# Message passing on a graph: the chunks of 8 tiles end at sorting step 36 instead of 140

## The chip, the cores and the metric

The kernel runs on one core of a Trainium2 chip. Its engines work side by side, each through its own list of instructions in order: TensorE (PE; its weight loads are shown as PEld), VectorE (DVE), ScalarE (ACT), GpSimd (POOL, which here issues the indirect DMAs) and SyncE (SP, which issues the plain DMAs). They wait for one another through semaphores. The metric is the time of one execution on the device in microseconds (us).

## The reference: what is computed

A graph has 12,500 nodes with 64 features and 800,000 edges with 16 features. Each edge takes the features of its source, of its destination and its own, multiplies them with a weight matrix, and applies SiLU; the messages are summed by destination, and each node is updated from its features and its sum.

```python
m_in = jnp.concatenate([x[src], x[dst], e_attr], axis=-1)
msg = _silu(m_in @ w_msg)
agg = _segment_sum(msg, dst, N)
return _silu(jnp.concatenate([x, agg], axis=-1) @ w_upd)
```

Sources and destinations are drawn at random, so edges come in no order, and the sum is by destination.

## The kernel before, in words

**Two halves that run side by side.** The first half sorts edges by destination into 128 buckets of 98 nodes. A tile is 128 edges; there are 6250 of them. The sorted records (17 numbers: 16 edge features, and one that packs source and position) go to a store in device memory, `st`. The second half reads whole tiles of one bucket back, forms the messages, and adds them into the accumulator `ACC`.

**Sorting step.** There are 782 steps of 8 tiles (`M`). A step goes through a pipeline of periods, one stage a period: `onehot` (ACT makes a one-hot matrix of the buckets, lines 396 and 397) and `sums` (running sums over the tiles of a chunk, lines 403 to 412, mostly DVE); then `count` (PE, lines 425 to 428, into the only PSUM tile `z`), `ranks` (DVE, line 433: each edge's rank in its bucket) and `expand` (DVE, lines 442 to 446: each record is put at its rank's place in a wide row of `X`); then `move` (PE, line 463: one-hot matrix times `X`, which adds the tiles of a chunk up in the only PSUM tile `pl`). When a chunk is complete, ACT copies the block out (line 468), and `place` (DVE, lines 481 and 482) moves the buckets' pointers on. In the period after, POOL scatters the block to the store (line 486), one row to each bucket.

**Chunks.** A chunk is the set of tiles whose ranks are counted together and which make one scatter. The first `K8 = min(N8, ...)` chunks have 8 tiles, one step and one scatter each (`turn` 3). All later chunks have 12 tiles: three steps hold two chunks, and `turn` 0, 1, 2 says which of the three a step is. A row of `X` for the tile at position n of its chunk has room for `LIM[n]` records, so that the moving operand of line 463 has `2 + 17 * LIM[n]` columns, and the scattered row of a bucket has the room of the chunk's last tile:

```python
LIM = [k for k in (13, 17, 21, 24, 27, 30) for _ in range(2)]
S = LIM[-1]
S8 = LIM[M - 1]
```

That gives 223, 223, 291, 291, 359, 359, 410, 410 columns for a chunk of 8, and 461, 461, 512, 512 more for the last four tiles of a chunk of 12. In turn 1 a chunk ends after the step's fourth tile: `move(0)` does four tiles, then comes the product of the other half, then `move(1)` does four tiles of the next chunk. The running sums go on over the border of a step inside a chunk of 12: turns 0 and 2 need two additions (lines 409 and 410) where a chunk of 8 has one (412), and turn 2 needs a third count matmul for both of its halves (line 428); the others need it for one.

**Groups and batches.** The second half works on groups of tiles, and a group is fed to the pipeline in batches. A group takes units of `u` tiles of one bucket, and there are three stages, by the line

```python
FIRST = [(1, 48, BT, (1, 0, 1, 0)), (2, 24, 6, (3, 3, 2, 2))]
```

First units of 1 in batches of 8 (64 tiles in all), then units of 2 in groups of 24 and batches of 6 (640 tiles), then units of 4 (`QU`) in groups of 64 and batches of 8; in the end units of 1 for what is left, and the last, part-filled tiles. A group is formed over several periods: DVE works out from the pointers which tiles it takes (`fourth`, lines 545 to 563), with two small PE passes (`middle`, lines 581 and 585 to 587), then SP loads the tiles from the store into `rt` (line 569), and DVE takes the indices out (`fifth`, line 530). For the groups of the first two stages (`quick`) the first PE pass stands inside the period's main stream: PE waits there for DVE's `wl`. A batch then takes one period for each of: `gather` (POOL, line 649: one indirect DMA a tile fetches the sources' rows into one of four buffers `g`) and its one-hot matrix (DVE 659, ACT 660); `transpose` (PE 668, ACT 671) and `product` (PE 677); `message` (DVE 681, ACT 682); `reduce` (PE 698) and `add` (DVE 706 or 710).

**The order of work.** The order within a period is written out by hand in `period` (lines 715 to 773): POOL gets four gathers, then the scatter, then the rest of the gathers; PE gets `count`, `transpose`, `reduce`, `move(0)`, `product`, `move(1)`; DVE gets the batch's one-hot, `ranks`, `message`, `add`, `sums`, `expand`, `place`.

**The planner.** When a group may begin is decided when the program is made, with no knowledge of the data. `Draws` keeps sixteen drawn examples of how full the buckets are, from a generator with a fixed seed; `holds` asks whether the least full of them has enough whole units; `place(Chunk(i).m)` adds a chunk's tiles to them when the chunk is placed. A period for which no group is ready has no batch. When all steps are done, the remaining batches run alone, at the end.

The number of chunks also sets how many tiles of the store each bucket owns (`CAPT`), where the last chunk's empty tiles lie (`T1`, `GAP`), and the size of the table `LOST`, which would list chunks where a bucket had more records than room; such chunks would be done again at the end.

Of the kernel before, what the change touches and what calls it, by code (L numbers as in the profile page):

```python
# [21 lines left out]
MAGIC = 12582912.0  # L22
M = 8
C = 12
N8 = 140
LIM = [k for k in (13, 17, 21, 24, 27, 30) for _ in range(2)]
S = LIM[-1]
S8 = LIM[M - 1]
# [20 lines left out]
def mpnn_kernel(tc, x, e_attr, src, dst, w_msg, w_upd, out):  # L49
# [4 lines left out]
    assert E % P == 0 and NB <= NBK and NT >= C  # L54
    K8 = min(N8, NT // (2 * M))
    NCH = K8 + (NT - K8 * M + C - 1) // C
# [1130 lines left out]
```

## Time and profile before

| what | value |
|---|---|
| median of 3 runs | 10888.96 us (10887.72 to 10916.87) |
| the profiled execution's own time | 10887.83 us |
| its span | 10886.0 us |
| the last sorting step's rank reduction starts | 10036.8 us |
| gathers, scatters | 6322, 567 (and one to another pointer) |
| busy share of the span: PE, DVE, ACT, POOL | 82%, 66%, 47%, 60% |

The profile is one execution. Times are counted from the start of its span. A row for a stretch gives its length, then each engine's busy time and the number of its instructions in it, then the mean TensorE clock that was granted (1.00 is full), the DMA engines' busy share and GB/s; where the row is of one line's instructions, the engines' times are of these alone. A row of a group gives line, engine, operation, output and inputs, shapes, count, busy time and mean duration in ns, and then the engine's idle time just before, with what ended it. A row in order of time gives start, duration, engine, line, operation, how many were merged, and in brackets the idle time before it. Matmuls are pipelined, so that start to start tells more of them than a duration.

### The profile page before, as it was taken

Reading aid. Unit: us, or ns where it says so; the run is one execution under the profiler, and the core shown is the slowest. Engines: PE = TensorE matmul, PEld = TensorE weight load, DVE = VectorE, ACT = ScalarE, POOL = GpSimd, SP = SyncE. Lnnn points to the kernel's source line nnn. Section 1 sums busy time; section 2 is a strip of 40 time slices with the busy share of each in tenths; the row PEclk is TensorE's granted clock in tenths of the full one; section 3 lists DMA queues with packets and bytes.
Section 4 is the critical chain, followed back from the end, with each engine's and each line's share of the span. In section 5 each row is a group of like instructions: output and inputs, shape, how many; then the busy total and the mean of one; then the engine's idle time right before and its main releaser. Section 6 shows DMA issues by size and latency. Waiting matters only on the chain. (4 is left out here: it accounts for less than half of the span.)

```text
span 10886.0 us, 155616 instructions
## 1 busy us (share of the span) xinstructions
PE 8949.9 (82%) x49053; PEld 6219.2 (57%) x49816; DVE 7231.4 (66%) x15936; ACT 5082.6 (47%) x12594; POOL 6571.4 (60%) x6908
## 2 busy tenths in 40 slices
PE   8788888888888888888888888888888888888556
PEld 5566655555555555555555555555555555555555
DVE  7777776666666666766666666666666666766232
ACT  6455554444444444444444444444444444544211
POOL 2565666666666666666666666666666666666555
PEclk9999998999989988999998999999899998988555
DMA  3111111111111111111111111111111111111212
GB/s 97 44 49 48 49 49 46 43 47 42 47 42 46 45 44 45 44 43 44 46 43 46 44 44 43 46 47 43 45 42 46 43 47 44 44 45 41 46 36 44
DMA packets 662903, 501.15 MB, mean 46 GB/s; under 512 B 492983, under 2 KB 529911, under 8 KB 662071
## 3 DMA queue, kind: packets, MB, share of 16 engines
q0 software_dynamic: 238976, 349.72, 12.3%
q1 hardware_dynamic: 422775, 141.27, 5.9%
q8 instruction: 400, 6.55, 0.3%
q14 instruction: 432, 3.54, 0.1%
q10 hardware_dynamic: 320, 0.07, 0.0%
HBM read 330.05 MB, written 152.30 MB: 44 GB/s over the span
## 5 line engine op out<-in xcount | busy, mean ns | idle before, releaser
L649 POOL DMA_INDIRECT g<-A_d,sidx x6322 | 5997.6, 949 | 3658.7 <-issue 1620.7
L463 PE MATMUL pl<-X,hf 128*128 128x291 f32 (+5 forms) x12512 | 4745.0, 524 | 476.4 <-issue 428.3
L463 PEld LDWEIGHTS pl<-X,hf 128*128 128x128 f32 x12512 | 2538.7, 211 | 2159.4 <-issue 1737.4
L446 DVE TENSOR_TENSOR X<-cb,rec 128x442 f32<-128x442 f32 (+5 forms) x3128 | 2646.6, 908 | 26.7
L396 ACT ACTIVATE hf<-iof,shi 128x128 f32<-128x128 f32 x6256 | 1908.8, 389 | 1360.4 <-PE pl L463 449.0
L671 ACT ACTIVATE qt<-tq 114x1024 f32<-114x1024 f32 (+1 forms) x818 | 811.7, 992 | 2951.3 <-remote 2298.5
L433 DVE TENSOR_REDUCE rank<-z 128x8 f32<-128x1024 f32 x782 | 954.5, 1221 | 1270.3 <-remote 874.9
L677 PEld LDWEIGHTS pre<-w,qt 114*128 114x128 f32 x10496 | 1392.5, 209 | 687.8 <-ACT qt L671 467.1
L677 PE MATMUL pre<-w,qt 114*128 114x64 f32 x10496 | 1395.2, 291 | 345.6 <-ACT qt L671 317.6
L710 DVE TENSOR_TENSOR ACC<-ag,ACC 64x98 f32 x1938 | 496.7, 256 | 1553.3 <-remote 1131.7
L698 PE MATMUL ag<-q,g 128*64 128x98 f32 x12644 | 882.3, 276 | 490.4 <-remote 236.2
L698 PEld LDWEIGHTS ag<-q,g 128*64 128x64 f32 x12644 | 681.6, 151 | 668.8 <-issue 381.7
L668 PE MATMUL tq<-ident,q 128*114 128x128 f32 x6322 | 929.9, 294 | 103.3 <-issue 91.5
L668 PEld LDWEIGHTS tq<-ident,q 128*114 128x114 f32 x6322 | 812.6, 147 | 238.7 <-issue 122.6
L397 ACT ACTIVATE hf<-hf,ones 128x1024 f32<-128x1024 f32 x782 | 898.8, 1149 | 25.4
L486 POOL DMA_INDIRECT st<-blk,ptrs x567 | 567.2, 1000 | 561.4 <-ACT blk L468 272.2
L659 DVE TENSOR_TENSOR q<-cb,lo 128x784 f32<-128x784 f32 (+1 forms) x818 | 768.7, 940 | 96.1 <-PE ag L698 46.3
L468 ACT ACTIVATE blk<-pl 128x512 f32<-128x512 f32 (+1 forms) x568 | 324.9, 572 | 818.2 <-PE pl L463 500.9
L426 PE MATMUL z<-G,onesb 128*128 128x384 bf16 x1564 | 529.8, 339 | 78.9 <-issue 25.2
L682 ACT ACTIVATE g<-g 128x512 f32<-128x512 f32 (+1 forms) x818 | 498.4, 609 | 192.5 <-DVE g L681 111.8
L681 DVE TENSOR_TENSOR g<-pre,g 128x512 f32<-128x512 f32 (+1 forms) x818 | 541.3, 662 | 51.4 <-issue 37.2
L677 PE MATMUL pre<-BW,qt 114*128 (+1 forms) x2148 | 326.3, 314 | 99.0 <-ACT qt L671 64.8
(138 smaller groups left out, 5243.9 us busy)
## 6 DMA issues: line engine op xcount, KB each, us to landing
g<-A_d,sidx POOLq DMA_INDIRECT x6322
ea<-in_e_attr SPq DMA_DIRECT2D x260, 192.0 KB
rt<-st SPq DMA_DIRECT2D x1312, 34.0 KB
st<-blk,ptrs POOLq DMA_INDIRECT x567
rt<-st SPq DMA_DIRECT2D x434, 8.5 KB
nodes<-in_x SPq DMA_DIRECT2D x62, 98.0 KB
ACC<-rt SPq DMA_DIRECT2D x11, 544.0 KB
rt<-st SPq DMA_DIRECT2D x320, 17.0 KB
```

The costliest lines, as they stand in the source:

```text
L396: nc.scalar.activation(c.hf[:, k, :], iof, AF.Square, bias=c.hi[:, k:k + 1])
L397: nc.scalar.activation(c.hf, c.hf, AF.Relu, bias=ones, scale=-1.0)
L433: nc.vector.tensor_reduce(out=c.rank, in_=c.z, axis=AX.X, op=OP.max)
L446: nc.vector.tensor_tensor(out=c.x[:, k:k + 2, 2:2 + n * R].rearrange("p k (s c) -> p k s c", c=R), in0=hit[:, k:k + 2, 0:n, None].to_broad ...
L463: nc.tensor.matmul(pl[:, 0:w], c.hf[:, k, :], c.x[:, k, 0:w], start=(n == (c.size - 1 if whole else 0)), stop=ends, skip_group_check=True)
L486: i = nc.gpsimd.indirect_dma_start(out=st, out_offset=bass.IndirectOffsetOnAxis(ap=c.ptr, axis=0), in_=c.blk[:, 2:], in_offset=None)
L649: j = nc.gpsimd.indirect_dma_start(out=t.g[:, i, :], out_offset=None, in_=A_d, in_offset=bass.IndirectOffsetOnAxis(ap=t.grp.sidx[:, k:k + ...
L659: nc.vector.tensor_tensor(out=t.q[:, 0:n, 0:BK], in0=ioB[:, None, :].to_broadcast([P, n, BK]), in1=t.grp.lo[:, i0:i0 + n, None].to_broadca ...
L668: nc.tensor.transpose(t.tq[0:KQ, j * P:(j + 1) * P], t.q[:, j, :], ident)
L671: nc.scalar.activation(t.qt[:, 0:w], t.tq[0:KQ, 0:w], AF.Copy)
L677: nc.tensor.matmul(t.pre[:, i * D:(i + 1) * D], t.qt[:, i * P:(i + 1) * P], w, start=True, stop=True)
L698: o = nc.tensor.matmul(t.ag[t.half(v), v // 2 * BK:(v // 2 + 1) * BK], t.g[:, i, :], t.q[:, i, 0:BK], start=(k == 0), stop=(k == u - 1))
```

## The change

`N8`, the number of chunks of 8 tiles at the start, goes from 140 to 36:

```diff
 M = 8
 C = 12
-N8 = 140
+N8 = 36
 LIM = [k for k in (13, 17, 21, 24, 27, 30) for _ in range(2)]
```

Steps 0 to 35 stay as they were. Steps 36 to 139 now belong to chunks of 12 and go through turns 0, 1 and 2, as the later steps do. There are 533 chunks instead of 568, and so 35 scatters fewer. The steps are 782 as before; the last one has 4 tiles. A bucket owns 125 tiles of the store instead of 128, and `LOST` has 533 columns. The planner's draws are made in other portions.

## The prediction

> **What bounds the kernel now.** I read the page first (engine shares, slices), then tables by stretches of time with the instructions of one line alone, then lists in order of time. The page names no single full engine:
>
> ```profile
> span 10886.0 us, 155616 instructions
> PE 8949.9 (82%) x49053; PEld 6219.2 (57%) x49816; DVE 7231.4 (66%) x15936; ACT 5082.6 (47%) x12594; POOL 6571.4 (60%) x6908
> ```
>
> The change touches the sorting steps 36 to 139, so the stretch that matters is found by counting steps. Each sorting step has one rank reduction (L433). Its rows for three stretches (the stretch, its length, busy time, count, granted TensorE clock, DMA share, GB/s):
>
> ```profile
> 600.00:1400.00 800.00, 87.64 (x72) 0.92 0.20 49
> 1700.00:9700.00 8000.00, 735.12 (x602) 0.91 0.17 45
> ...
> 355.80:1519.40 1163.60, 126.57 (x105) 0.92 0.20 50
> ```
>
> A step takes 800/72 = 11.1 us in the first stretch, where chunks have 8 tiles, and 8000/602 = 13.3 us in the second, where they have 12. The third stretch runs from the reduction of step 36 to that of step 140: 104 steps, 11.2 us each. These are the steps that the change rewrites. It is tempting to say that each will then cost 13.3 us (104 x 2.1 = +218 us), but the two stretches differ in something else too, the gathers (L649):
>
> ```profile
> 600.00:1400.00 800.00, 410.13 (x431) 0.92 0.20 49
> 1700.00:9700.00 8000.00, 4564.05 (x4814) 0.91 0.17 45
> ```
>
> 431/72 = 6 gathers a step early, 4814/602 = 8 later: the early batches belong to the second stage of groups, with 6 tiles a batch, and that stage is not touched. So the change makes a kind of step that the profile hardly has: chunks of 12 with batches of 6. What the two extra tiles cost must come out of the 2.1 us.
>
> All engines over the same two stretches (length; PE, PEld, DVE, ACT, POOL busy):
>
> ```profile
> 600.00:1400.00 800.00, 665.30 (x3734) 487.28 (x3806) 612.01 (x1607) 418.56 (x1031) 482.17 (x503) 0.92 0.20 49
> 1700.00:9700.00 8000.00, 6745.60 (x36911) 4577.32 (x37513) 5492.84 (x11580) 3859.84 (x9629) 4966.48 (x5216) 0.91 0.17 45
> ```
>
> In the early stretch PE is busy 83% and VectorE 77% of the time: PE leads, VectorE is close behind. ScalarE (52%) has room.
>
> **The change part by part.** *TensorE, the moves (L463).* A move of 8 tiles sends 2 x (223+291+359+410) = 2566 columns; three moves with chunks of 12 send 2 x 2 x (223+291+359+410+461+512) = 9024, or 3008 each: 442 more a step. PE in order of time, two early steps with chunks of 8 (start, us, line, count):
>
> ```profile
> 1096.57 4.58 PE L463 MATMUL pl<-X,hf 128*128 128x410 f32 x16
> 1100.99 1.45 PE L677 MATMUL pre<-BW,qt 114*128 x12
> ...
> 1103.06 0.38 PE L428 MATMUL z<-G,onesb 128*128 128x512 bf16 x1
> 1103.27 0.82 PE L668 MATMUL tq<-ident,q 128*114 128x128 f32 x6
> 1104.02 0.89 PE L698 MATMUL ag<-q,g 128*64 128x98 f32 x12
> 1104.84 4.58 PE L463 MATMUL pl<-X,hf 128*128 128x410 f32 x16
> ```
>
> The move starts at 1096.57 and the product at 1100.99: 4.42 us, 1.72 ns a column; 442 more columns are 0.76 us. The crossover at step 140 has, for a moment, what the change makes common, three moves of chunks of 12 beside batches of 6:
>
> ```profile
> 1536.87 3.53 PE L463 MATMUL pl<-X,hf 128*128 128x461 f32 x8
> 1540.24 1.45 PE L677 MATMUL pre<-BW,qt 114*128 x12
> 1541.53 1.95 PE L463 MATMUL pl<-X,hf 128*128 128x223 f32 x8
> 1543.32 0.39 PE L425 MATMUL z<-hf,w 128*128 128x512 bf16 x1
> ...
> 1545.65 6.11 PE L463 MATMUL pl<-X,hf 128*128 128x359 f32 x16
> 1551.60 1.00 PE L677 MATMUL pre<-BW,qt 114*128 x8
> ```
>
> From start to the next start: 3.37 + 1.79 = 5.16 us for the second move of a turn, 5.95 for the third; the first has the columns of a chunk of 8 (4.42). Mean 5.18, again 0.76 more. The split move also shows that waiting for the only `pl` buffer between its halves is hidden behind the product.
>
> *TensorE, the counts.* One step in three has a third-term matmul (L428) more; 1103.06 to 1103.27 is 0.21 us, a third is 0.07. TensorE: **+0.83 us a step**. As a check, two more tiles cost 2 x (0.75/6 + 1.29/6 + 0.82/6) = 0.95 us by the starts above, and 0.83 + 0.95 = 1.8 of the 2.1 us between the two kinds of step. So step time follows TensorE's work.
>
> *VectorE.* The expansions (L446), by the same two stretches, and the small groups, over the whole run (count | busy us, mean ns):
>
> ```profile
> 600.00:1400.00 800.00, 214.99 (x286) 0.92 0.20 49
> 1700.00:9700.00 8000.00, 2086.87 (x2408) 0.91 0.17 45
> ```
>
> ```profile
> L412 DVE TENSOR_TENSOR G<-G,hf 128x128 bf16<-128x128 bf16 x568 | 174.3, 307 | 19.5
> ...
> L409 DVE TENSOR_TENSOR cb<-G,hf 128x128 f32<-128x128 bf16 x428 | 126.8, 296 | 7.3
> L482 DVE SCALAR_TENSOR_TENSOR ptrs<-blk,LOST,ptrs 128x1 int32<-128x1 f32 x567 | 125.9, 222 | 20.1
> L410 DVE TENSOR_TENSOR G<-cb,G 128x128 bf16<-128x128 f32 x428 | 124.6, 291 | 14.6
> ...
> L481 DVE SCALAR_TENSOR_TENSOR LOST<-blk 128x1 f32<-128x1 f32 x568 | 86.9, 153 | 95.9 <-ACT blk L468 83.3 <-issue 11.8
> ```
>
> Four expansions a step: 214.99/286 x 4 = 3.01 us against 2086.87/2408 x 4 = 3.47: +0.46. Running sums: one L412 (0.307) becomes two thirds of L412, L409 and L410 each, 2/3 x 0.894 = 0.596: +0.29. A third of the L481 and L482 pairs goes: -0.125. VectorE: **+0.63 us a step**. One block copy in three goes from ScalarE; it has room, so this counts nothing.
>
> *POOL.* 69 or 70 of 104 scatters stay, 35 go. POOL in order of time:
>
> ```profile
> 1109.05 0.94 POOL L649 DMA_INDIRECT g<-A_d,sidx  x1 [2.00 <-remote]
> ...
> 1114.06 1.00 POOL L486 DMA_INDIRECT st<-blk,ptrs  x1 [0.30 <-issue]
> ```
>
> A scatter holds POOL for 1.00 + 0.30 us (the pause before each), a gather for about 0.95 + 0.30, so a step loses 0.43. POOL's work in an early step is 6 x 1.25 + 1.30 = 8.8 of 11.1 us, and each batch's first gather waits (2.00 us here), so I book nothing; if POOL were the bound, this would be a gain of 45 us (a rival below). The scatters' bytes fall too (two thirds of 2040 against 1632 bytes a partition), in DMA engines with a 0.20 share: nothing.
>
> *Waits.* No wait is added. The group that is being formed makes PE wait for VectorE's `wl` once in a group (PE in order of time):
>
> ```profile
> 1115.91 0.38 PE L581 MATMUL cb<-wl,tri 128*128 128x1 f32 x2 [3.94 <-DVE wl L546]
> ```
>
> Groups have 24 tiles, 4 batches of 6, so this is one step in four. There VectorE's chain sets the end, and it grows by 0.63; in the other three PE's 0.83 counts. Mean (3 x 0.83 + 0.63)/4 = 0.78 us; **104 x 0.78 = +81 us**. Ends for one step: -0.43 (POOL bounds all) and +1.56 (below); I take 0.78 as it lies at the rows of the stage itself.
>
> *The plan of groups.* The planner sees no run-time data: its draws come from a generator with seed 1. Worked through by its own arithmetic for 140 and 36, both have 847 periods and 818 batches, and the same 29 periods without a batch (0 to 24, 33 to 36), so no batch moves to the end. Two differences: two groups of the second stage begin at steps 49 and 51, not 47 and 49, and the last group of 64 tiles with a unit of 4 becomes one with a unit of 1. The first may let VectorE wait for loads into `rt`; all such waits of 117 groups are 13.8 us:
>
> ```profile
> L530 DVE CAST sidx<-rt 128x64 int32<-128x64 f32 x117 | 33.5, 286 | 33.7 <-DMA rt<-st 13.8 <-issue 13.5 <-DMA g<-A_d,sidx 3.3
> ```
>
> I take +3 (0 to 13.8). The second is priced by the message additions (L681) in the tail, units of 4 and then of 1:
>
> ```profile
> 10070.00:10260.00 190.00, 9.64 (x14) 0.55 0.23 47
> 10280.00:10860.00 580.00, 30.40 (x45) 0.57 0.23 40
> ```
>
> 13.6 us a batch against 12.9: 8 batches, -5 us (0 to -10). The last step has 4 tiles instead of 8: half a move, -3. By the inputs as they are drawn no bucket of any chunk passes its limit before or after (after twelve tiles at most 28 of 30), so the path for lost records does not run.
>
> *Sum.* 81 + 3 - 5 - 3 = +76 us on the profiled execution's 10887.83, which stands 1.1 below the median of 10888.96: **10965 us**.
>
> **A rule beside a row.** PE's wait of 3.94 us has a tail. Before it and just after it (columns as for all engines):
>
> ```profile
> 1089.40:1116.60 27.20, 23.07 (x136) 17.18 (x138) 21.69 (x51) 15.74 (x40) 17.81 (x19) 1.00 0.26 66
> 1116.60:1120.00 3.40, 3.40 (x18) 2.38 (x17) 1.29 (x4) 0.89 (x2) 1.35 (x2) 0.50 0.12 24
> ```
>
> For 3.4 us the granted clock is 0.50, which costs 1.7 us of TensorE time. The Trainium skill, "TensorE: Matmul & The Clock Gate", section on what is actually happening in Part 1, says that the clock falls to half after an idle window of about 3.4 us and comes back after a busy one, and that the windows run freely. The trace agrees in size and place. It is a mechanism by which more TensorE work could cost less (third rival).
>
> **Rivals.** *POOL is what steps wait for* (faster). For it: the two kinds of step differ by two gathers, 2 x 1.25 - 0.43 = 2.1 us of POOL, as well as 1.8 us of PE. Against it: POOL itself waits at a batch's first gather. It decides if those waits are only a shadow of POOL's own lateness; then 104 x -0.43 = -45: 10844. *It is hidden*: PE is idle 17% of the stage, 1.9 us a step, and 0.8 could go into that: about 10885. Against it: the waits are for VectorE, which gets more work too. *Fewer half-clock windows*: PE's wait falls by 0.83 - 0.63 = 0.20, to 3.7 us; if that makes it miss a window in each of 26 groups, 26 x 1.7 = 44 us come back: 10921. *The move is slower than its columns say.* L463 over the two stretches (PE busy, PEld busy):
>
> ```profile
> 600.00:1400.00 800.00, 355.22 (x1148) 224.56 (x1149) 0.92 0.20 49
> 1700.00:9700.00 8000.00, 3800.97 (x9628) 1968.01 (x9629) 0.91 0.17 45
> ```
>
> 4.95 against 6.32 us a step, +1.37, and with the counts about +1.56: 104 x 1.56 = +162, 11050. Against it: the crossover's moves had their plain length. *The change doesn't do what it says*, in that steps stay without a batch: each would add about 13 us at the end; the plan above has none.
>
> **How the numbers follow.** Chances: forecast 0.67 (10935 to 10995 by itself), slower move 0.08, fewer windows 0.07, hidden 0.11, POOL 0.07. A change of 0.3% (33 us) is about what a measurement of this kernel tells from none. Faster is POOL, 0.07; same is hidden and a part of fewer windows, 0.13; slower is the rest, 0.80. The range leaves out POOL, the lower half of hidden, and most of slower move: 10890 to 11010.
>
> **What would show it.** Right: the 104 steps take 11.9 to 12.0 us; scatters fall from 567 to 532; early moves average 5.2 us from start to next start; L409 and L410 appear before 1400 us; the stage with 8 tiles a batch stays at 13.3. Wrong: early steps at 10.8 (POOL), at 11.2 (hidden), or above 12.5, or a later stretch whose steps change.

## The result, and the profile after

The changed kernel takes 10919.3 us (median of 14 runs, 10891.79 to 10941.12) beside 10901.2 for the kernel before (14 runs): a ratio of 1.0014, with a 95% interval of 1.0004 to 1.0024. That is 15 to 18 us where 76 were forecast: less than the 0.3% that the prediction names as what a measurement tells from none, though inside the range given. The profiled execution took 10907.74 us. The head of its page:

```profile
span 10905.8 us, 155764 instructions
## 1 busy us (share of the span) xinstructions
PE 8991.1 (82%) x49079; PEld 6205.4 (57%) x49842; DVE 7300.5 (67%) x16020; ACT 5068.6 (46%) x12543; POOL 6526.7 (60%) x6873
```

PE and DVE have more to do, POOL less, as the change says. The rewritten steps 36 to 139, all engines over the stretch (length; PE, PEld, DVE, ACT, POOL busy; granted clock, DMA share, GB/s), first the kernel before, then the changed one:

```profile
355.80:1519.40 1163.60, 964.66 (x5381) 703.83 (x5483) 885.58 (x2324) 605.45 (x1490) 704.69 (x735) 0.92 0.20 50
```

```profile
357.70:1514.50 1156.80, 1016.24 (x5406) 692.08 (x5508) 949.67 (x2354) 598.67 (x1456) 668.95 (x700) 0.93 0.21 47
```

Here the sum of the prediction falls. PE has 52 us more to do, DVE 64, POOL 36 less, and the 104 steps take 11.1 us each: 7 us *less* in all, where +81 was forecast. What the whole loses, it loses after the last step. The gathers (L649) from the last rank reduction on, in three stretches (length, POOL busy, count), before and after:

```profile
10036.80:10086.80 50.00, 30.26 (x32) 0.76 0.14 34
10086.80:10286.80 200.00, 113.44 (x120) 0.55 0.24 49
10286.80:10886.00 599.20, 334.59 (x354) 0.57 0.23 40
```

```profile
10018.80:10068.80 50.00, 18.31 (x20) 0.83 0.15 40
10068.80:10268.80 200.00, 112.68 (x120) 0.54 0.22 39
10268.80:10905.80 637.00, 349.66 (x371) 0.59 0.26 41
```

This tail took 849.2 us and now takes 887.1. In its first 250 us the changed kernel starts 140 gathers, the kernel before 152. With +2 before step 36 and -13 between step 140 and the last one, +2 - 7 - 13 + 38 = +20 is the difference of the two profiled spans.

### The profile page after: what moved, and what is told of

Its sections match the earlier page's. It is cut to its first block, busy times and chain, and to the rows that moved or that the text cites. A ratio compares the mean times of both kernels' runs of the same rounds, so it can differ in the third digit from the quotient of the medians.

```text
span 10905.8 us, 155764 instructions
## 1 busy us (share of the span) xinstructions
PE 8991.1 (82%) x49079; PEld 6205.4 (57%) x49842; DVE 7300.5 (67%) x16020; ACT 5068.6 (46%) x12543; POOL 6526.7 (60%) x6873
## 5 line engine op out<-in xcount | busy, mean ns | idle before, releaser
L649 POOL DMA_INDIRECT g<-A_d,sidx x6322 | 5988.9, 947 | 3723.2 <-issue 1648.6
L463 PE MATMUL pl<-X,hf 128*128 128x410 f32 (+5 forms) x12504 | 4802.1, 529 | 467.4 <-issue 428.7
L446 DVE TENSOR_TENSOR X<-cb,rec 128x442 f32<-128x442 f32 (+5 forms) x3126 | 2692.8, 923 | 26.6
L433 DVE TENSOR_REDUCE rank<-z 128x8 f32<-128x1024 f32 x782 | 954.0, 1220 | 1121.4 <-remote 780.9
L486 POOL DMA_INDIRECT st<-blk,ptrs x532 | 531.2, 999 | 556.9 <-ACT blk L468 276.1
```

Source lines behind the costliest of these rows:

```text
L433: nc.vector.tensor_reduce(out=c.rank, in_=c.z, axis=AX.X, op=OP.max)
L446: nc.vector.tensor_tensor(out=c.x[:, k:k + 2, 2:2 + n * R].rearrange("p k (s c) -> p k s c", c=R), in0=hit[:, k:k + 2, 0:n, None].to_broad ...
L463: nc.tensor.matmul(pl[:, 0:w], c.hf[:, k, :], c.x[:, k, 0:w], start=(n == (c.size - 1 if whole else 0)), stop=ends, skip_group_check=True)
L649: j = nc.gpsimd.indirect_dma_start(out=t.g[:, i, :], out_offset=None, in_=A_d, in_offset=bass.IndirectOffsetOnAxis(ap=t.grp.sidx[:, k:k + ...
```

## The experiments

A word ahead, since it decides how the numbers are read. The runs were made in sets, each set on one chip, and the sets are of two kinds. In three of them the kernel before took 10720, 10894 and 10728 us, like the first measurement (10901); in two others the same kernel took 8912 and 8926. I call a chip of the first kind late and one of the second early, for a reason that is shown further down. The names stand for what was seen in a set: the sets at 10894 and at 8912 us are on record under the same chip number. Ratios are always to the kernel before in the same set, and stages are compared within one kind, between sets in which the kernel before took about the same time.

**The tail alone.** Two kernels exchange the last group of 64 tiles and nothing else. First the changed kernel with the group of units of 4 kept (5952 tiles up to there), then the kernel before without it (5888):

```diff
-        large = work["used"] + max(0, draws.sure(QU) * QU // GT * GT) if state["u"] == QU else 0
+        large = 5952
...
+        large = 5888
```

> The changed kernel, but the last group of 64 tiles with units of 4 is kept (93 groups up to there, as before the change), so that one group of units of 1 goes. Theory 'the tail costs it': the stretch from the last rank reduction (849.2 us before the change, 887.1 after) falls by 25 to 40 us to about 850, and the time to about 10880, 20 below the kernel before; steps 36 to 139 stay at 11.1 us. Rival 'the tail differs by chance or by its starting state': it stays at 870 to 890 us and the time at about 10919.

> The kernel before (N8 = 140), but its last group of 64 tiles with units of 4 is given up for one with units of 1, as the change does. Theory 'the tail costs it': the stretch after the last rank reduction rises from 849 to about 885 us, the time to about 10937, and steps 36 to 139 stay at 11.2 us. Rival 'chance or starting state': 850 us and 10901.

The first stood at 1.0007 (0.9997 to 1.0018) with a tail of 852.1 us, the second at 1.0026 (1.0016 to 1.0036) with a tail of 865.0. On the same kind of chip, the one other kernel with chunks of 8 and the group of units of 4 (it leaves out gathers in early steps, next part) had 829.2, and the changed sorting with units of 1 had 864.6 and 864.2. So giving the group up costs the kernel before +28 us by its ratio and 36 by these two tails; keeping it gives the changed kernel back only some 12 to 18 us (852.1 and 846.3 against 864). What keeps its tail 17 to 23 above 829 was not separated; in the sets near 10900 us, three profiles of chunks of 8 with that group differ by 12 us among themselves (849.2, 857.6, 861.2).

**POOL and its transfers.** The scatters that go had been booked at nothing. One kernel gives the changed one a gather in each period that lost its scatter, into a buffer that nobody reads; another takes a gather away from every third early step of the kernel before (the second part of the diff):

```diff
+            elif q and 38 < flow["ic"] <= 142:
+                nc.gpsimd.indirect_dma_start(out=GX, out_offset=None, in_=A_d, in_offset=bass.IndirectOffsetOnAxis(ap=q.grp.sidx[:, q.i0:q.i0 + 1], axis=0))
...
+                    if i == 5 and 38 < flow["ic"] <= 142 and flow["ic"] % 3 == 0:
+                        continue
```

> The changed kernel with POOL's lost work put back: in steps 36 to 139 each period without a scatter issues one more indirect gather, of 128 rows into a buffer that nobody reads. Theory 'the scatters that go pay for the added TensorE and VectorE work' (POOL and PE take turns as the bound): steps 36 to 139 rise from 1156.8 us by 30 to 45, to 1187 to 1202 (11.4 to 11.6 a step). Rival 'the added work lies in TensorE's idle time and POOL plays no part': 1152 to 1163 us (11.1 a step).

> The kernel before, where in one of three of the steps 36 to 139 the batch's sixth gather is left out (that tile then takes an older batch's rows, so its messages are not the reference's): POOL loses as much work as by the scatters that the change removes, and nothing is added elsewhere. Theory 'POOL paces these steps': 1163.6 us fall by 30 to 43, to 1120 to 1134 (10.8 to 10.9 a step). Rival 'POOL does not pace them': 1158 to 1168 us (11.2 a step).

The all-engine rows of the stretch from the reduction of step 36 to that of step 140: chunks of 12 without the added gathers (the kernel with 5952, whose early steps are those of the changed kernel) and with them,

```profile
357.60:1494.10 1136.50, 1011.23 (x5513) 684.66 (x5512) 949.79 (x2355) 598.11 (x1452) 669.80 (x700) 0.95 0.21 47
```

```profile
356.40:1525.50 1169.10, 1019.05 (x5511) 686.69 (x5511) 949.89 (x2354) 598.64 (x1455) 701.41 (x734) 0.94 0.22 47
```

and chunks of 8 with all their gathers (the kernel with 5888) and with 35 fewer:

```profile
356.50:1496.10 1139.60, 965.27 (x5478) 701.91 (x5477) 884.82 (x2323) 604.51 (x1490) 703.71 (x735) 0.91 0.23 51
```

```profile
358.50:1464.40 1105.90, 953.31 (x5480) 695.82 (x5479) 883.51 (x2323) 606.52 (x1490) 673.51 (x700) 0.92 0.23 51
```

+32.6 us and -33.7 us, just under 1 us for each of some 35 transfers; the times agree (1.0052, where the changed kernel itself stands at 1.0014 and 1.0019 in other sets, and 0.9972 for the one that leaves gathers out). It looked as if POOL paced the stage. The next set tested that with work on POOL that transfers nothing.

**TensorE's part alone, VectorE's part alone, and POOL's time without a transfer.** The first two parts of the diff are two kernels made from the kernel before: one sends the first tile of each move (410 columns) twice, one expands the first pair of tiles twice. The third part goes into the changed kernel, in the periods that lost their scatter.

```diff
+                    if whole and k == M - 1 and 38 < flow["ic"] <= 142:
+                        nc.tensor.matmul(pl[:, 0:w], c.hf[:, k, :], c.x[:, k, 0:w], start=True, stop=False, skip_group_check=True)
...
-                for k in range(0, c.n, 2):
+                for k in (0, *range(0, c.n, 2)) if 38 < flow["ic"] <= 142 else range(0, c.n, 2):
...
+            elif q and 38 < flow["ic"] <= 142:
+                for _ in range(4):
+                    nc.gpsimd.memset(sent, 0.0)
```

> The kernel before, with TensorE's part alone: in steps 36 to 139 each move sends the 410 columns of its first tile twice (0.70 us a step at 1.72 ns a column, 73 us in all); nothing else changes. Theory of the prediction ('PE sets the end of three steps in four'): steps 36 to 139 take 50 to 55 us more than without it. Theory 'POOL paces them': 0 to 10 us more. Theory 'shared' (the pace is a loop through PE, DVE and POOL, in which each one's work counts in part): 15 to 35 us more, with PE's idle time falling by 40 or more.

> The kernel before, with VectorE's part alone: in steps 36 to 139 the expansion of the first pair of tiles is done twice (0.6 us a step, about 64 us in all); the values are the same. Theory of the prediction (VectorE sets the end of the step in which a group is formed, one in four): 16 us more in steps 36 to 139. Theory 'POOL paces them': 0 to 10. Theory 'shared': 10 to 30 us more, and together with TensorE's part about 30 to 45, which is what the 35 scatters that go (about 33 us by the last runs) pay back.

> The changed kernel as it is, beside the kernel before and the others of this call on one chip. It should stand 0.1 to 0.2% above the kernel before; steps 36 to 139 within 10 us of the kernel before, and the stretch after the last rank reduction 15 to 40 us longer. If that stretch is not longer here, the difference of the two first profiles was chance.

> The changed kernel with POOL's time put back without a transfer: in steps 36 to 139 each period without a scatter does four memsets of 128x272 on POOL, about 1.3 us. Theory 'POOL's time counts': as with the added gather, 25 to 40 us more in steps 36 to 139 than the changed kernel. Theory 'the transfers count, not the engine': 0 to 10 us more.

The same rows, in this order: PE's part, DVE's part, the changed kernel as it is, the changed kernel with memsets.

```profile
359.00:1521.90 1162.90, 1006.88 (x5586) 728.84 (x5688) 885.71 (x2323) 608.40 (x1490) 703.63 (x735) 0.94 0.22 50
```

```profile
358.70:1536.50 1177.80, 957.24 (x5375) 698.12 (x5478) 942.24 (x2427) 610.74 (x1491) 704.23 (x735) 0.92 0.22 49
```

```profile
360.30:1525.40 1165.10, 1020.57 (x5412) 694.58 (x5515) 950.70 (x2354) 597.23 (x1452) 668.29 (x700) 0.93 0.21 46
```

```profile
357.20:1495.60 1138.40, 1007.01 (x5406) 683.12 (x5507) 949.15 (x2355) 598.00 (x1456) 714.66 (x839) 0.95 0.21 47
```

Against the 1163.6 us of the kernel before: some 73 us of TensorE work (104 times 410 columns at 1.72 ns) cost nothing (1162.9; ratio 0.9995, 0.9986 to 1.0004). In the row it appears as 42 us more PE time at a mean clock of 0.94, not 0.92. By the clock records of the two traces, PE was busy at half clock for 170 us of the stage before and for 111 here. So about 42 of the 73 us went into PE's idle time, and about 30 came back because less of the work ran at half clock. VectorE's 57 us more cost 14 in the stage (1.0017, 1.0007 to 1.0027, for the whole). That is a quarter, as if they counted in one step of four, but two profiles of the changed kernel differ by 8 us there (1156.8 and 1165.1), so the share is rough. The changed kernel stands at 1.0019 (1.0009 to 1.0030) with a tail of 875.8 us. The memsets, 46 us more of POOL's time, cost nothing; the stage even came out 27 us shorter, and the whole at 1.0001. So "POOL paces them" falls: on these chips POOL's time did not count here, its transfers did.

**A scatter put back, the order of the tiles, two repairs at once, memsets in the kernel before.** The first sends the block before once more to a buffer `sx` in device memory; the second lets a chunk of 8 send its tiles first to last; the third is the changed kernel with 5952 and the memsets; the fourth has the memsets in the kernel before, in one period of three, ahead of the fifth gather.

```diff
+                prior["s"] = s
+            elif q and 38 < flow["ic"] <= 142:
+                nc.gpsimd.indirect_dma_start(out=sx, out_offset=bass.IndirectOffsetOnAxis(ap=ptrx, axis=0), in_=prior["s"].blk[:, 2:], in_offset=None)
...
-                whole = c.turn == 3
+                whole = c.turn == 3 and not 38 < flow["ic"] <= 142
...
+            if q and 38 < flow["ic"] <= 142 and flow["ic"] % 3 == 2:
+                for _ in range(4):
+                    nc.gpsimd.memset(sent, 0.0)
```

> The changed kernel with a scatter put back in each of the periods of steps 36 to 139 that lost one: the block before is sent once more, 128 rows of 2040 bytes, to a buffer in device memory that nobody reads. POOL and the transfers are then as before the change or a little above it; the chains of the blocks (TensorE, ScalarE, VectorE) stay as the change has them. Theory 'the scatters that go pay for VectorE's added work': steps 36 to 139 take 12 to 35 us more than the changed kernel (1157 and 1165 us). Rival 'what pays is on the path from the move to the next group (no block copy and no pointers in one step of three), or fewer half-clock windows, not the scatters': within 8 us of the changed kernel.

> The kernel before, with chunks of 8, but from step 36 on a move sends its tiles in the order first to last, as the chunks of 12 do, not last to first; so it can start on the first pair's expansion while VectorE still expands the later ones. Theory 'the order of the tiles is part of what the change gains': TensorE's idle time before the moves (21 us in steps 36 to 139) falls to under 5, and the steps together by 8 to 20 us. Rival 'that idle time lies in the shadow of others': the idle time goes and the steps stay within 6 us of 1163.

> The changed kernel with two repairs together: the last group of units of 4 is kept, and POOL does the four memsets in steps 36 to 139 where no scatter is. If both effects are real and add, the tail falls by 20 to 28 us and the steps by 20 to 28 us against the changed kernel, and the time is 20 to 30 us below the kernel before (ratio about 0.998). If one of the two was chance, it stands within 10 us of the kernel before.

> The kernel before, with the same four memsets on POOL in one period of three of steps 36 to 139 (between the fourth and the fifth gather). POOL's work rises by 45 us. Theory 'POOL has room, and work on it without a transfer costs nothing': within 8 us of 1163. Theory 'a pause before the last two gathers helps by itself, whatever the chunks': 15 to 27 us less. Theory 'POOL paces the stage': 30 to 45 us more.

This set fell on an early chip: the kernel before took 8911.6 us. There the first came to 1.0096 (1.0079 to 1.0113), with 1019.4 us for the steps 36 to 139; the second to 1.0001 (0.9992 to 1.0011), 925.2 us; the third to 1.0098 (1.0081 to 1.0115), 1017.3 us; the fourth to 1.0049 (1.0032 to 1.0066), 964.5 us. All expectations had been written for the other kind of chip, and nearly all miss. The order of the tiles made no difference there; on a late chip it was not run. But with chunks of 12 the stage was suddenly 92 us longer than with chunks of 8, about what the prediction had said. The next set asked whether that is the change itself: the kernel before, the changed kernel, and the first and third kernel of this set again.

> The kernel before itself, for a profile beside the others of this call. On a chip where TensorE's completions reach the other engines about 4 us late (as in the first profile: VectorE's rank reduction starts 4.0 us after the end of the count's rows): steps 36 to 139 take 1140 to 1165 us, the whole 10700 to 10900. On one where they arrive at once (as in the last call): 920 to 930 us, 8.9 a step, with POOL never idle, the whole about 8910.

> The changed kernel. Theory 'TensorE sets the steps where its completions arrive at once, and its waits hide the added work where they arrive late': on an early chip steps 36 to 139 take 1015 to 1020 us, 92 more than the kernel before (TensorE's 86 and what POOL no longer hides), and the whole stands 1.0 to 1.3% above it; on a late chip they take 1137 to 1165 and the whole stands 0.1 to 0.2% above it. Rival 'the difference of the last call came from what was put into the kernels there, memsets and scatters': on an early chip within 30 us of the kernel before.

> The changed kernel with a scatter put back in each period of steps 36 to 139 that lost one, a second time. On an early chip: as measured, 1019 us in these steps, no more than the changed kernel, since TensorE sets them. On a late chip, theory 'the scatters that go pay for VectorE's added work': 12 to 35 us above the changed kernel of this call. Rival 'they do not': within 8 us of it.

> The changed kernel with the last group of units of 4 kept and with memsets on POOL in the periods without a scatter, a second time. On an early chip: steps as the changed kernel (1017), so it differs from it by the tail alone; if the group of units of 1 costs there too, it stands 10 to 30 us below the changed kernel, and if that cost comes from late completions, within 8 us. On a late chip: 35 to 50 us below the changed kernel, ratio to the kernel before about 0.998.

Again an early chip (kernel before 8925.6 us). The changed kernel as it is stands at **1.0096** (1.0079 to 1.0112), 85 us above; with scatters 1.0099 (1.0082 to 1.0115), with the two repairs 1.0093 (1.0076 to 1.0110). The head of the page of the kernel before, and the stage, kernel before, then changed:

```profile
span 8921.8 us, 155616 instructions
...
PE 8171.7 (92%) x49053; PEld 5887.4 (66%) x49816; DVE 7248.9 (81%) x15936; ACT 5060.5 (57%) x12594; POOL 6595.1 (74%) x6908
```

```profile
323.70:1248.60 924.90, 872.20 (x5360) 652.78 (x5461) 873.39 (x2325) 596.10 (x1488) 703.84 (x726) 1.00 0.27 62
```

```profile
323.70:1339.20 1015.50, 955.66 (x5390) 654.85 (x5492) 945.01 (x2354) 591.69 (x1450) 671.54 (x699) 1.00 0.23 53
```

DVE, ACT and POOL have the same work as on the late chip to within 0.5%, and the kernel is done 18% sooner. Steps 36 to 139 take 8.9 us with chunks of 8 and 9.8 with chunks of 12: +90.6 us in all, of which 83.5 is PE's busy time (94% of the stage in both). The tail is 692.7 and 691.9 us: the loss of the late chips is not there.

What differs between the kinds is seen where an engine waits for PE. The rank reductions of the stretch, kernel before on the late chip and on the early one (after the bar: busy, mean ns; idle time before them and what ended it):

```profile
L433 DVE TENSOR_REDUCE rank<-z 128x8 f32<-128x1024 f32 x105 | 127.8, 1217 | 112.6 <-remote 94.1 <-PE ag L698 13.2 <-PE z L428 2.6
```

```profile
L433 DVE TENSOR_REDUCE rank<-z 128x8 f32<-128x1024 f32 x105 | 127.4, 1213 | 3.1 <-PE z L428 2.6
```

And one of them in order of time on the late chip:

```profile
700.21 0.38 PE L428 MATMUL z<-G,onesb 128*128 128x512 bf16 x1
700.43 0.82 PE L668 MATMUL tq<-ident,q 128*114 128x128 f32 x6
701.17 0.89 PE L698 MATMUL ag<-q,g 128*64 128x98 f32 x12
...
702.50 4.56 PE L463 MATMUL pl<-X,hf 128*128 128x410 f32 x16 [0.43 <-DVE X L446]
...
705.95 1.22 DVE L433 TENSOR_REDUCE rank<-z 128x8 f32<-128x1024 f32 x1 [2.47 <-remote]
```

The count's last row ends at 700.59, and the reduction that waits for nothing but the count starts at 705.95, after 2.47 us of idle time: 5.4 us late. PE has gone on to the transposes, the reduce and the move meanwhile. The other steps show the same. Where VectorE stood idle before the reduction in these 104 steps (more than 0.15 us), it started a median of 3.9 us after the end of the count's last row on this late chip (48 steps) and 0.04 us after it on the early one (12 steps); in the other profiles the medians are 2.6 to 4.3 us on late chips and again 0.04 on early ones. Hence late and early: on the one kind PE's results reach the others microseconds after its rows end, on the other at once.

The trace also records when PE raises its semaphore. For the nine of these rows of the count, the transposes and the reduce that raise it, with ends from 700.37 to 702.06, the raisings stand at 705.89 to 706.25, about 0.04 us apart; the move's last row ends at 707.05, and its raising stands at 707.07. A move of 4.56 us does not fit between 706.25 and 707.07, so PE was at work on it while the earlier results were still unreported. In these rows it is the report that is late, not the work.

**The scatters and the two repairs once more.** The last set fell on a late chip again (kernel before 10728.4 us).

> The changed kernel with a scatter put back in each period of steps 36 to 139 that lost one, a third time, in the hope of a chip on which TensorE's completions arrive late. There the changed kernel's steps took 1157 and 1165 us (kernel before at 10900) or 1137 (kernel before at 10720). Theory 'the scatters that go pay for VectorE's added work': 12 to 35 us above that. Rival: within 8 us. On an early chip again 1017 to 1019, which decides nothing.

> The changed kernel with the last group of units of 4 kept and memsets on POOL in the periods without a scatter, a third time. On a late chip: 35 to 50 us below the changed kernel, ratio to the kernel before about 0.998, if both effects are real and add. On an early chip again a ratio of about 1.0095.

```profile
357.40:1527.40 1170.00, 1021.34 (x5510) 687.89 (x5509) 949.24 (x2355) 596.76 (x1452) 701.05 (x734) 0.94 0.24 54
```

With the scatters back, 1170.0 us against 1136.5 for chunks of 12 and 1139.6 for chunks of 8 on the same kind of chip: the 35 scatters that the change drops are worth 33 us, and without that the stage would be 30 us longer than before the change. The ratio agrees (1.0053, 1.0035 to 1.0071). The two repairs came to 1.0003 (0.9991 to 1.0015), steps 1130.7 us, tail 846.3: about the kernel before, not below it. The gain of the memsets did not come back in its first size (6 us against the 1136.5, not 27). No kernel that I tried and that computes the reference's result is clearly faster than the kernel before.

## Why the prediction was wrong

*TensorE, +0.83 us a step.* As an amount of work this was right: on the early chip PE's busy time in the 104 steps grew by 83.5 us, 0.80 a step. The step that failed is "in the other three PE's 0.83 counts", which makes up nearly all of the +81. On late chips, where the forecast was made, 73 us of such work alone cost nothing. I had read "PE busy 83%, so PE leads" from the shares and had checked it with "step time follows TensorE's work"; but that check compared two kinds of step which differ in PE, POOL and batches alike, and does not tell a work-bound step from one that is bound by hand-overs. The rival "it is hidden" described most of what happened, but I had held its waits against it because they end with VectorE.

*VectorE, +0.63 us a step.* Right as work (+64 us) and, on late chips, about right in its share: 14 measured for 57 us alone.

*POOL, -0.43 us a step, booked as 0.* This term failed too. On late chips the scatters that go are worth 33 us, and with them the 104 steps come out at -7, +2 (changed kernel 1156.8 and 1165.1 against 1163.6) and -3. The rival "POOL bounds" had nearly the size, but not the reason: memsets of the same length cost nothing there. The parts tested alone (0 + 14 - 33 = -19) do not add up to these; 12 to 21 us are left over, and where they come from is open. Chunks of 12 also send their tiles first to last, chunks of 8 last to first; on a late chip this was not tested by itself.

*The tail, -5 us.* It was the likely cost, not the gain: +27 on the chip kind of the forecast (856 mean of three profiles with units of 4, 883 of three with units of 1). I had priced eight batches by the spacing of later, steady ones, and not the change from one group to the next. Shortly before that change the four scatters that close the buckets (L995) hold up the gathers. POOL in order of time, changed kernel:

```profile
10047.83 0.94 POOL L649 DMA_INDIRECT g<-A_d,sidx  x1 [0.30 <-issue]
10054.44 1.00 POOL L995 DMA_INDIRECT st<-X,pe  x1 [5.67 <-DVE done L1002]
10058.08 0.97 POOL L995 DMA_INDIRECT st<-X,pe  x1 [2.64 <-DVE ACC L710]
10065.80 0.96 POOL L995 DMA_INDIRECT st<-X,pe  x1 [6.75 <-DVE q L659]
10069.45 0.96 POOL L995 DMA_INDIRECT st<-X,pe  x1 [2.69 <-DMA st<-X,pe]
10070.72 0.97 POOL L649 DMA_INDIRECT g<-A_d,sidx  x1 [0.30 <-issue]
```

From 10047.83 to 10070.72 no gather is issued: three of the closing scatters wait for work on DVE that stands behind the batches, the fourth for the transfer of one before it. The same four stand in the kernel before, where they hold the gathers for 18 us, so this is at most a small part of the loss. A larger part comes at the change itself, when the gathers of the first group of units of 1 should begin. A group of 64 tiles in units of 1 needs 64 loads into `rt`, sixteen a period; one in units of 4 needs 16 in all (2114 loads in the whole run instead of 2066). The changed kernel again, from lists of SP, DVE and POOL:

```profile
10148.23 12.61 SPq L569 DMA_DIRECT2D rt<-st  x16
...
10162.48 0.21 DVE L530 CAST sidx<-rt 128x64 int32<-128x64 f32 x1 [8.26 <-DMA XU_d<-nodes]
...
10149.86 0.94 POOL L649 DMA_INDIRECT g<-A_d,sidx  x1 [0.30 <-issue]
10163.43 0.94 POOL L649 DMA_INDIRECT g<-A_d,sidx  x1 [12.62 <-issue]
```

The last sixteen loads of the group are issued until 10160.8; DVE takes out the indices only after that, and POOL stands still for 12.6 us. (The profile puts the end of DVE's wait down to another transfer of the same queue; in two of the other profiles it names the loads themselves.) The same gap, 9.9 to 13.0 us, is in all six late profiles without the group of units of 4, and at this place in none of the six with it; the early profile of the changed kernel does not have it. DVE's idle time before L530 in the whole tail is 25.3 us in the changed kernel and 10.3 in the kernel before, so some 15 us of the loss stand here; the rest was not separated.

*Fewer half-clock windows.* This rival was seen at about half of its 44 us: the mean clock of the stage goes from 0.92 to 0.93, and to 0.94 with PE's part alone. By the traces' clock records PE's busy time at half clock falls from 170 us to 124 and 126 in the two profiles of the changed kernel, which is worth half the difference, some 22 us of TensorE time.

*The rest.* Scatters fell to 532, the first additions of the kind L409 and L410 stand before 1400 us, the stage with 8 tiles a batch stayed at 13.3 us a step (573 reductions in 7600 us): as forecast. The 104 steps at 11.1 to 11.2 was named as the sign of "hidden".

On an early chip the same working gives nearly the right number: +76 forecast, +85 measured (9010.8 against 8925.6), +91 in the stage. There the kernel before is at the end of POOL's work: a gather takes 0.95 + 0.30 and a scatter 1.00 + 0.30, 8.8 us a step, and a step takes 8.9; the 45 us of memsets in one period of three cost 40 (against 924.9 without them):

```profile
323.10:1287.60 964.50, 892.47 (x5358) 666.14 (x5461) 877.35 (x2324) 595.46 (x1488) 743.61 (x859) 0.98 0.26 59
```

With chunks of 12 PE takes over at 9.2 us of 9.8, and then neither scatters (1017.4) nor memsets (1017.3) cost more than 2 us against 1015.5. So the near match there is in part luck: the prediction held that POOL is no bound, and before the change it was one.

Behind "PE's 0.83 counts" stood an assumption that the prediction does not spell out: that a row's end is the moment at which others may go on. The rows of the profile it was made from showed the opposite, in the idle time of L433, "remote", which I passed over. That this lateness is what makes added TensorE work free is inferred from the two kinds of chip, where the one goes with the other; no run changed the lateness alone. The POOL and tail terms failed beside it, each for itself.

The Trainium skill, "Perfetto Trace Analysis", section on the Tensor Engine instruction, says that the end of a matmul in a profile is computed from its size, and that the semaphore is pushed only when PSUM has acknowledged the writes. The traces agree that the two can differ, and give the size: 5.4 us in the rows above, a median of 3.9 in the stage, and 0.04 on the early chip.

## What to carry to other kernels

Before you call an engine the bound by its busy share, look at a consumer that waits for it, and compare the consumer's start with the end of the row that it waits for; where microseconds lie between, added work on the producer may be free, and the steps follow the chain of hand-overs. Price a change of the group plan by what is queued at the seam (who waits, and what stands behind it), not by the steady spacing on either side. And where a kernel is near several limits at once, the same edit can be nothing in one set of runs and 1% in the next: measure on both kinds before you keep it.

## What the hardware showed that was not expected

- The same program took 10720 to 10901 us in some sets of runs and 8912 to 8926 in others, with the same busy time on DVE, ACT and POOL. The mean TensorE clock over the run was 0.885 and 0.939. One chip number is on record with both kinds, so the number alone does not decide it; what does, the runs do not tell.
- On the late kind, some 35 transfers issued by POOL, added or taken away, moved the stage by 33 us whether they were gathers or scatters, though POOL waited before a gather some 100 times in the 104 steps, while four memsets of 0.33 us each in the same place added nothing. What a transfer holds up there is open; that PE's late results and these transfers share a resource was not tested.
